# A new written-out order of steps and other filler products, in a kernel of banded attention and a Mish layer

## The chip, the cores and the metric

The kernel runs on one core of a Trainium2 chip. The metric is the time of one execution on the device in microseconds (us). TensorE multiplies matrices, VectorE (DVE), ScalarE (ACT) and GpSimd (POOL) work on elements, and SyncE (SP) issues the loads and stores to the DMA engines. Each engine works through its own list of instructions in order, and waits in that list for what it needs from others.

## The reference

```python
B, H, S, D = 8, 8, 576, 64                       # q, k, v
scores = q @ k^T / sqrt(D)                       # heads 0-3: the last 32 keys
scores = where(mask, scores, -1e9)               # heads 4-7: every 4th of the last 128 keys
attn = softmax(scores) ; attn_out = attn @ v
x = attn_out as [B*S = 4608, H*D = 512]
h = x @ w_in                                     # 512 x 2048
g = h * tanh(log1p(exp(min(h, 20))))             # or h*tanh(h) above 20
out = g @ w_out                                  # 2048 x 512
```

The weights are 64-bit numbers: each of the two is 8 MB in HBM, and is loaded as integers and turned into a pair of f16 numbers (a high and a low half) on the chip.

## The kernel before

The work is cut into 16 units (u = 0 to 15), half a sequence of 288 rows each. The attention of a unit is small: scores of two kinds (0 plain band, 1 dilated), 72 and 96 f32 products of 64 by 32 by 64; exponentials; transposes; values in three parts; division; transposes of x. Units 0 to 2 ("direct") take their values as f32 and transpose on TensorE, later ones work with pairs of f16 and transpose by DMA. The hidden layer of a unit is eight steps of 24 products (128 x 128 by 288), each in two halves of 12. The output layer of units 0 to 2 is 16 steps of 12 products; for later units it is replaced by seven products of sums of quarters, on sums of w_out that VectorE makes once (su, gq, ga, fq).

The weights come in half groups of 1024 KB: w_in's group g as wl0.g.0 and wl0.g.1, w_out's as wl1.g.0 and wl1.g.1. Each half group goes through a maximum (wm on ACT or POOL, ws on TensorE and VectorE), through its words (ww: POOL, then VectorE twice) and through the split (wp: ACT, then VectorE). Four buffers hold loaded halves; w_in's group 1 goes straight into the room of w2.

Every step is a generator function that issues a piece of work, yields, and goes on when its name comes again. The order of all instructions is a list written out by hand of some 2120 names, ORDER (L41 to L175), which the loop at L1012 follows; a planner outside of the kernel has searched it. Each engine's list of instructions is what this loop issues to it, in that order. "=2" behind a name tells which of the buffers in turn is taken. The names, with the function and its lines: ld loads q, then k, then two halves of the dilated keys (loads, L455); lv loads values, plain and dilated in turn, first a memset for direct units (loads_v, L484); qp copies q (L481); sp, sc, ex, tp, va, tx are scores, maximum, exponential, transpose, values, transpose of x (L551, L580, L611, L637, L668, L717); pr finds the scale of v (L510); wl, wm, ws, ww, wp are the weights (L340 to L424); ff is a step of the hidden layer (L781); fo one of the output layer (L964); kw and kh multiply fillers.

In sc the units 0 and 1 subtract the maximum by a product on TensorE (L604). In lv the dilated values go by one DMA per window s into interleaved places of one tile (L503 to L506):

```python
for s in range(ns):
    row = vd[b, 0, half * (RB - K0) + s * step, 2 * a * D:2 * (a + 1) * D]
    nc.sync.dma_start(o[:, n0:].rearrange("k (r s) n -> k r s n", s=ns)[:, :, s],
                      bass.AP(row.tensor, row.offset, [[w, WK], [2 * RB * w, NR], [1, 2 * D]]))
```

The fillers multiply ones into a spare corner of PSUM that nobody reads, "kw" n times in f32 (two products each), "kh" n times in bf16 (one each):

```python
def keep_warm(n, one=ones):
    for _ in range(n):
        nc.tensor.matmul(spare, one.broadcast_to([P, P]), one.broadcast_to([P, WIDE_MAX]), start=not spared, stop=True, skip_group_check=True)
```

## Time and profile before

| what | before |
|---|---|
| median of 3 runs | 860.55 us (857.65 to 860.93) |
| the profiled execution | 862.81 us, span 860.9 us |
| TensorE busy | 842.1 us, 98% of the span |
| VectorE, ScalarE, GpSimd busy | 636.1, 477.8, 96.0 us |
| mean granted clock of TensorE | 0.992 |
| DMA, mean over the span | 100 GB/s |

The span runs from the first to the last instruction of the profile. "PE" is TensorE's products, "PEld" its weight loads, "SPq" the load queue of SyncE. A granted clock of 1.00 is 2.4 GHz, 0.50 is 1.2 GHz. A record in an engine's timeline may hold many instructions of one line; in brackets stands the idle time ahead of it and what ended it, and "issue" means that the engine waited for nothing that the profile shows. A few records of products are missing.

### The profile page before, as it was taken

Reading aid. Unit: us, or ns where it says so; the run is one execution under the profiler, and the core shown is the slowest. Engines: PE = TensorE matmul, PEld = TensorE weight load, DVE = VectorE, ACT = ScalarE, POOL = GpSimd, SP = SyncE. Lnnn points to the kernel's source line nnn. Section 1 sums busy time; section 2 is a strip of 40 time slices with the busy share of each in tenths; the row PEclk is TensorE's granted clock in tenths of the full one; section 3 lists DMA queues with packets and bytes.
Section 4 is the critical chain, followed back from the end, with each engine's and each line's share of the span. In section 5 each row is a group of like instructions: output and inputs, shape, how many; then the busy total and the mean of one; then the engine's idle time right before and its main releaser. Section 6 shows DMA issues by size and latency. Waiting matters only on the chain.

```text
span 860.9 us, 32197 instructions
## 1 busy us (share of the span) xinstructions
PE 842.1 (98%) x14818; PEld 727.3 (84%) x14821; DVE 636.1 (74%) x818; ACT 477.8 (55%) x615; POOL 96.0 (11%) x99
## 2 busy tenths in 40 slices
...
GB/s 270 213 151 266 154 146 87 73 144 130 70 57 13 126 80 178 57 144 96 126 67 102 69 150 76 131 72 102 94 73 109 43 127 18 57 40 34 1 22 37
DMA packets 154887, 86.29 MB, mean 100 GB/s; under 512 B 92288, under 2 KB 150656, under 8 KB 154752
## 3 DMA queue, kind: packets, MB, share of 16 engines
...
q8 instruction: 116, 1.90, 1.0%
...
## 4 chain that ended last, share of the span: by engine, by line
PE 86%; DMA 7%; DVE 3%; SPq 2%; ACT 1%; issue 1%; POOL 0%; DVEq 0%; POOLq 0%; ACTq 0%
PE b L790 40%; PE b L933 31%; PE b L972 8%; DMA vf<-in_vd 4%; PE b L689 4%; PE b L577 3%; DMA raw<-in_w_in 2%; DMA knd<-in_kdT 1%; DVE g L903 1%; SPq L348 1%; DVE hm L909 0%; DVE w L424 0%; SPq L501 0%; PE b L385 0%; ACT g L901 0%
## 5 line engine op out<-in xcount | busy, mean ns | idle before, releaser
L790 PE MATMUL b<-x,w 128*128 128x288 f16 x3072 | 393.4, 286 | 0.2 <-ACT hm L796 0.2
L790 PEld LDWEIGHTS <-w 128*128 128x128 f16 x3072 | 295.4, 98 | 75.5 <-issue 0.6
L903 DVE SCALAR_TENSOR_TENSOR g<-hm,sg,g 128x1152 f16<-128x1152 f32 (+1 forms) x104 | 131.3, 1272 | 53.7 <-ACT g L901 52.9
L933 PE MATMUL b<-g,w 128*128 128x144 f16 x2496 | 164.9, 226 | 0.8 <-issue 0.7
L933 PEld LDWEIGHTS <-w 128*128 128x128 f16 x2496 | 158.4, 98 | 3.2 <-issue 1.1
L796 ACT ACTIVATE hm<-b,fs 128x576 f32<-128x576 f32 x128 | 92.8, 738 | 113.5 <-PE b L790 99.2
L901 ACT ACTIVATE g<-hm,sg 128x1152 f16<-128x1152 f32 (+1 forms) x104 | 116.0, 1127 | 40.1 <-PE b L933 26.4
L481 POOL COPY qp<-qn 128x576 f32<-128x576 f32 x15 | 34.9, 2326 | 433.6 <-DMA qn<-in_qT 317.9
L909 DVE TENSOR_TENSOR hm<-hm 128x576 f32<-128x576 f32 x104 | 79.0, 763 | 1.9 <-ACT hm L796 0.4
L972 PE MATMUL b<-g,w 128*128 128x288 f16 x576 | 73.3, 286 | 0.1
L947 ACT ACTIVATE y<-b,fo 128x288 f32<-128x288 f32 x52 | 40.6, 786 | 58.9 <-PE b L933 57.6
L972 PEld LDWEIGHTS <-w 128*128 128x128 f16 x576 | 55.6, 98 | 14.4 <-DVE w L424 0.3
L952 DVE SCALAR_TENSOR_TENSOR y<-b,fo,y 128x144 f32<-128x144 f32 x78 | 33.6, 478 | 45.8 <-PE b L933 22.7
L933 PE MATMUL b<-g,g 128*128 128x144 f16 x936 | 66.6, 226 | 0.3 <-DVE y L952 0.2
L933 PE MATMUL b<-g,late_sums 128*128 128x144 f16 x936 | 65.9, 226 | 0.0
L933 PEld LDWEIGHTS <-g 128*128 128x128 f16 x936 | 60.6, 98 | 2.2 <-issue 0.6
L933 PEld LDWEIGHTS <-late_sums 128*128 128x128 f16 x936 | 60.0, 98 | 0.5
L727 ACT CAST x<-xs 96x512 f16<-96x512 f32 (+1 forms) x39 | 26.7, 686 | 30.9 <-DMA x<-x 17.1
L729 DVE TENSOR_TENSOR x<-xs,x 96x512 f16<-96x512 f32 (+1 forms) x39 | 30.1, 772 | 16.6 <-ACT x L727 16.4
L545 DVE SCALAR_TENSOR_TENSOR vh<-vn,s,vh 128x2688 f16<-128x2688 f32 (+1 forms) x13 | 35.2, 2705 | 8.6 <-ACT vh L543 8.6
L705 DVE TENSOR_TENSOR xs<-b,rec 96x512 f32<-96x512 f32 (+1 forms) x48 | 37.2, 776 | 4.4 <-DVE rec L703 0.5
L689 PEld LDWEIGHTS <-pT 64*32 64x32 f16 (+1 forms) x3276 | 30.2, 90 | 5.3 <-issue 3.6
(127 smaller groups left out, 821.1 us busy)
## 6 DMA issues: line engine op xcount, KB each, us to landing
...
```

The source lines that it names most:

```text
L481: nc.gpsimd.tensor_copy(qp.rearrange("p (b r i) -> p b r i", r=NR, i=SQ // NR), d["q"][:, :2 * HT].rearrange("p (b i r) -> p b r i", r=NR, ...
L545: nc.vector.scalar_tensor_tensor(lo, src, s, hi, ALU.mult, ALU.subtract)
L689: nc.tensor.matmul(avv[s * SQ:(s + 1) * SQ, a, t - t0, h * (D + 1):(h + 1) * (D + 1)], p, vv[vi][ks, v0:v0 + D + 1], start=(i == 0), stop= ...
L705: nc.vector.tensor_tensor(xs.rearrange("p (a t h e) -> p a t h e", a=2, h=2, e=D), avv[:, :, :, 1:AW - 1].rearrange("p a t (h e) -> p a t ...
L790: nc.tensor.matmul(ph[:, h, :HT], w1[j][:, c, wi, k * P:(k + 1) * P], x_of(d, xi, c), start=(n == 0), stop=(n == len(seq) - 1))
L796: nc.scalar.activation(d["m"][p][:, half, k0:k0 + 2], ph[:, :, :HT], AF.Mish, scale=d["fs"][:, j:j + 1])
L901: nc.scalar.activation(hi, src, AF.Identity, scale=sg)
L903: nc.vector.scalar_tensor_tensor(lo, src, sg, hi, ALU.mult, ALU.subtract)
L909: nc.vector.tensor_tensor(a, a, b, op=op)
L933: nc.tensor.matmul(acc[e], left(l, e, p, wi)[:, k * P:(k + 1) * P], right(gi, k), start=(n in opens and p == 0 and q == 0), stop=(last and ...
L947: nc.scalar.activation(into(half, t), by(acc), AF.Identity, scale=fo)
L972: nc.tensor.matmul(po[:, :HT], w2[:, e, j, wi, k * P:(k + 1) * P], d["g"][j][:, gi, k, :], start=(j == 0 and n == 0), stop=(j == NCH - 1 a ...
```

## The change

Only the text of ORDER is changed: 2122 names instead of 2123. All steps other than the fillers occur as often as before; they are listed in another order, with other buffers in turn. The fillers before are kw18, kh32, kw17, kw8, kw1, kw3 and kw1; after, they are kw6, kh102, kw1, kw2, kw2 and kw2. The front of both lists and their last lines:

```diff
@@ -39,139 +39,138 @@
 EPS = 1.0e-9
 
 ORDER = """
-ld0 ld0 wl0.3.0 lv0 mf cs0 qp0 ww0.3.0 xa0 cs1 wl0.3.1 xa1 kw18 kh32 sp0.0=0 wm0.3.0 ld0 mf lv0 ww0.3.0 ld0 wm0.3.0
-wl0.0.0 wm0.3.1 lv1 ww0.3.0 sp0.0 wl0.0.1 ww0.3.0 ww0.3.1 kw17 sp0.1=1 sc0.0 ww0.0.0 sp0.1 ww0.3.0 ww0.3.1 lv0
-ww0.3.1 ws0.3=2 sc0.1 wm0.0.0 ws0.3 lv0 ww0.0.0 ww0.3.0 ld1 ww0.0.1 ww0.0.0 sc0.0 sc0.1 wm0.0.1 ex0.0 ld1 wp0.3.1
-kw8 tp0.0=3 ww0.0.1 wp0.3.1 kw1 ws0.0=2 ex0.1 ld1 ws0.0 ww0.0.1 qp1 wp0.0.0 tp0.1=0 kw3 sp1.0=1 tp0.1 sp1.0 ld1 lv0
-sp1.1=2 sp1.1 lv1 wp0.0.1 wl0.1.0 tp0.0 wp0.0.0 sc1.0 sc1.0 sc1.1 pr0 sc1.1 pr0 va0.0=0 wl0.1.1 wp0.3.0 pr0=3 pr0
-ex1.1 va0.0 va0.1=3 ww0.1.0 va0.0 wp0.3.0 va0.1 ex1.0 va0.2=2 lv1 va0.2 lv1 va0.0 va0.1 tp1.1=1 va0.1 wl0.2.1
-wm0.1.0 va0.2 fs0.0 tx0.1=3 va0.0 va0.2 wm0.1.1 tp1.1 kw1 tx0.0=0 ww0.1.0 tx0.1 ww0.1.1 lv1 tx0.0 tp1.0=2 ww0.1.1
-tp1.0 tx0.2=1 tx0.1 wl0.2.0 ws0.1=2 tx0.2 tx0.0 ld2 tx0.2 ww0.2.1 ff0.6=3 ff0.6 wp0.0.1 ws0.1 wm0.2.1 ww0.1.1
-ff0.7=0 wp0.1.1 ff0.0=1 ww0.2.0 ff0.0 fs0.3 ww0.1.0 ff0.1=2 lv2 ff0.7 ww0.2.1 wp0.1.1 wp0.1.0 ww0.2.1 wl1.1.0 fs0.1
-wp0.1.0 ff0.0 pr1 ff0.1 lv2 ff0.7 ff0.6 ff0.1 va1.2=1 wm0.2.0 pr1 va1.2 va1.0=0 va1.0 ld2 va1.0 pr1=3 ld2 ff0.2=2
-ww1.1.0 pr1 va1.2 ff0.2 ww0.2.0 va1.2 va1.0 ws0.2=3 ww0.2.0 ff0.2 ff0.3=1 ws0.2 tx1.2=2 ld2 tx1.2 ff0.3 wp0.2.0
-va1.0 wp0.2.1 tx1.0=3 tx1.2 wp0.2.0 wp0.2.1 sp2.1=0 wm1.1.0 va1.1=2 sp2.1 ff0.3 wl1.1.1 va1.1 tx1.0 tx1.0 ff0.5=1
-ww1.1.1 va1.1 sc2.1 ff0.4=3 wm1.1.1 qp2 ft wl1.0.0 wl1.0.1 fs0.4 fs0.2 va1.1 ww1.1.0 wm1.0.0 ff0.5 ff0.4 tx1.1=0 fs1
-sp2.0=2 ff0.5 ww1.1.1 tx1.1 tx1.1 ff0.4 sp2.0 gt0.0=0 ff1.0=1 gt0.1=1 lv2 sc2.0 ws1.1=0 ww1.1.1 ww1.0.0 ff1.6=3
-ws1.1 lv2 ff1.7=2 ex2.0 ff1.7 wp1.1.1 wp1.1.1 gt0.2=2 gt0.0 ff1.0 ff1.2=0 gt0.3=3 gt0.3 ld3 ex2.1 ff1.6 wm1.0.1 lv2
-ld3 wl1.2.0 ww1.0.1 ff1.2 ff1.0 ww1.2.0 ff1.6 ff1.7 ww1.0.0 ff1.1=1 ww1.1.0 gt0.1 wp1.1.0 ld3 ff1.5=3 xa2 ff1.1
-ff1.1 ww1.0.0 ww1.0.1 tp2.0=2 wp1.1.0 wl1.2.1 tp2.0 ws1.0=1 gt0.2 ws1.0 ff1.5 wp1.0.0 tp2.1=2 ww1.0.1 ff1.2 wp1.0.0
-ff1.4=1 wm1.2.0 wp1.0.1 tp2.1 ff1.5 ff1.4 pr2 ff1.3=0 pr2 ww1.2.0 ff1.4 ff1.3 wm1.2.1 ww1.2.1 fo0.0.0=2 wp1.0.1
-wl1.3.0 ff1.3 ww1.2.1 wl1.3.1 ww1.3.0 pr2=3 wm1.3.0 fo0.0.1 ws1.2=1 va2.2=0 pr2 va2.1=3 fo0.0.2 ws1.2 fo0.0.3
-fo0.0.3 ww1.2.0 va2.2 va2.0=1 va2.0 va2.2 va2.0 va2.1 xa3 fo0.1.0 wm1.3.1 fo0.1.1 ww1.2.1 va2.1 fo0.1.2 wp1.2.0
-va2.0 fo0.1.3 wp1.2.1 gt1.0=4 va2.1 va2.0 fs2 gt1.3=5 fo0.0.3 ww1.3.1 gt1.1=6 wp1.2.0 fo0.2.0=3 ld3 fo0.1.3 tx2.1=1
-fo0.2.1 ww1.3.1 ww1.3.0 ws1.3=2 wp1.2.1 va2.2 tx2.0=0 ww1.3.0 ws1.3 tx2.0 fo0.2.2 qp3 tx2.2=2 ww1.3.1 tx2.0 fo0.2.3
-fo0.1.3 sp3.1=0 sp3.1 tx2.1 wp1.3.0 fo0.2.3 wp1.3.0 tx2.1 fo0.3.0 fo0.3.1 tx2.2 wp1.3.1 wp1.3.1 fo0.3.2 ol fo0.3.3
...
-fq14.6.1 ga15.0 gq15.0.3 fq15.1.0=0 fq14.6.1 ga15.1 ga15.0 gq15.1.0 fq15.0.1 fq14.4.1 ga15.1 gq15.0.2=0 fq15.1.1
-gq15.1.3=1 gq15.1.3 fq15.0.1 fq15.2.0 fq14.4.1 ga15.1 gq15.0.2 fq15.2.1 fq15.1.1 gq15.1.2=4 gq15.1.2 fq15.2.1
-fq15.3.0 fq15.3.1 fq15.3.1 fq15.4.0 fq15.5.0 fq15.5.1 fq15.4.1 fq15.5.1 fq15.4.1 fq15.6.0 fq15.4.1 fq15.6.1 fq15.6.1
-fq15.6.1
+wl0.0.1 mf wl0.0.0 ww0.0.1 ww0.0.0 cs1 ld0 ld0 lv0 wm0.0.1 wm0.0.0 ww0.0.1 qp0 wl0.3.0 kw6 kh102 sp0.0=0 cs0 mf ld0
+sp0.0 lv0 ww0.0.0 ws0.0=1 ww0.0.1 xa0 ld0 xa1 sc0.0 sc0.0 wm0.3.0 ww0.0.0 ex0.0 wl0.3.1 lv0 sp0.1=2 ws0.0 wm0.3.1
+wm0.3.0 ww0.3.0 sp0.1 ww0.3.0 wp0.0.1 ww0.3.0 lv0 tp0.0=3 sc0.1 tp0.0 wp0.0.0 ww0.3.0 ld1 ww0.3.1 ld1 sc0.1 ww0.3.1
+ex0.1 ld1 ww0.3.0 lv1 kw1 ws0.3=1 wp0.0.1 kw2 tp0.1=0 ld1 wp0.0.0 ws0.3 kw2 sp1.1=2 ww0.3.1 tp0.1 wp0.3.1 sp1.1
+ww0.3.0 sc1.1 qp1 lv0 sp1.0=3 wl0.1.0 kw2 sc1.1 wp0.3.1 sp1.0 va0.1=1 ex1.1 wm0.1.0 pr0 lv1 pr0 ww0.1.0 sc1.0 pr0=0
+wp0.3.0 pr0 va0.1 va0.1 va0.0=2 wl0.1.1 sc1.0 va0.0 ex1.0 va0.0 va0.0 va0.2=0 ww0.1.0 va0.2 va0.2 ww0.1.1 va0.1
+wm0.1.1 tp1.1=3 va0.0 tx0.1=1 wp0.3.0 tp1.0=2 tp1.1 tx0.0=3 va0.2 tx0.1 fs0.0 wl0.2.1 wm0.2.1 ww0.1.1 tx0.2=0 tx0.1
+lv1 lv1 tp1.0 tx0.0 tx0.0 ww0.2.1 ws0.1=2 tx0.2 tx0.2 ff0.0=1 ww0.2.1 ws0.1 ww0.1.0 ff0.7=3 ff0.1=0 wp0.1.0 wl0.2.0
+ww0.1.1 wm0.2.0 ff0.6=2 ff0.0 ff0.6 ww0.2.0 wp0.1.0 ww0.2.1 wp0.1.1 ff0.0 fs0.1 ww0.2.0 wp0.1.1 lv1 ld2 ff0.7 ff0.1
+ws0.2=1 ww0.2.0 fs0.3 ws0.2 lv2 ff0.7 ff0.2=3 ff0.2 va1.0=1 ft ff0.6 va1.0 va1.0 wp0.2.1 pr1 ff0.1 va1.2=2 pr1 ld2
+va1.2 ff0.2 pr1=0 ff0.3=3 pr1 va1.0 ff0.3 va1.2 va1.0 wl1.1.0 qp2 va1.2 wp0.2.0 ld2 tx1.0=0 wp0.2.1 ld2 tx1.0
+tx1.2=1 sp2.1=2 wm1.1.0 ff0.3 wl1.1.1 sp2.1 lv2 va1.1=3 tx1.2 wp0.2.0 va1.1 tx1.2 ff0.5=1 fs0.4 va1.1 fs0.2 ww1.1.0
+gt0.0=0 va1.1 gt0.1=1 tx1.0 ff0.5 wm1.1.1 wl1.0.0 ff0.4=3 ff0.4 gt0.3=2 sc2.1 tx1.1=0 ww1.1.1 ff0.4 sp2.0=2 gt0.3
+tx1.1 fs1 ff0.5 gt0.2=3 tx1.1 sp2.0 ff1.5=3 ww1.1.0 ld3 ff1.5 lv2 ww1.1.1 ff1.2=0 sc2.0 ex2.1 ws1.1=1 ff1.2 gt0.0
+ws1.1 wl1.0.1 tp2.1=2 lv2 ff1.2 ff1.3=1 ww1.1.1 ww1.1.0 gt0.2 ff1.3 wp1.1.0 wm1.0.0 ld3 lv2 wp1.1.0 ff1.0=0 xa2
+ww1.0.0 ww1.0.1 ff1.5 ex2.0 tp2.1 ff1.0 ww1.0.0 ff1.3 pr2 wm1.0.1 ww1.0.1 ff1.4=3 ff1.4 wl1.3.1 gt0.1 wp1.1.1
+ww1.0.0 ff1.0 ld3 ws1.0=2 ff1.1=1 ff1.7=0 ff1.4 wp1.1.1 ff1.7 ws1.0 gt1.2=4 ff1.6=3 ff1.6 tp2.0=2 ww1.3.1 pr2
+wp1.0.0 ff1.7 ff1.6 wp1.0.0 fo0.0.0=0 ww1.0.1 ff1.1 wl1.2.1 tp2.0 pr2=3 wp1.0.1 ff1.1 fo0.0.1 va2.0=2 gt1.2 va2.0
+va2.0 va2.2=1 ld3 wp1.0.1 gt1.1=5 pr2 va2.1=3 va2.2 va2.1 va2.0 wm1.3.1 gt1.0=6 qp3 va2.0 wl1.2.0 va2.1 fo0.0.2
+fo0.0.3 va2.2 tx2.0=2 fo0.0.3 ww1.3.1 va2.1 tx2.0 gt1.0 tx2.1=3 wl1.3.0 va2.2 gt1.3=7 tx2.0 fo0.1.0 tx2.2=1 tx2.2
+ww1.2.1 ww1.2.0 fo0.1.1 wm1.2.1 wm1.2.0 tx2.2 sp3.1=2 ww1.3.0 fo0.0.3 tx2.1 sp3.1 tx2.1 ff2.2=1 sc3.1 gt1.1 ff2.0=3
+fo0.1.2 ww1.2.1 ff2.2 ww1.3.1 fs2 ff2.0 gt1.3 wm1.3.0 ld4 ww1.2.0 fo0.1.3 ff2.2 ex3.1 fo1.0.0=2 ww1.2.1 ff2.0
+fo1.0.1 fo0.1.3 ws1.2=1 ww1.3.0 ww1.3.0 ws1.2 fo1.0.2 ww1.2.0 fo1.0.3 wp1.2.0 fo1.0.3 ff2.3=3 ws1.3=0 ff2.1=1 ws1.3
+wp1.3.0 ff2.1 ff2.6=0 ff2.1 ff2.3 ff2.7=1 wp1.2.0 fo1.0.3 ff2.6 wp1.3.0 ff2.7 wp1.2.1 wp1.3.1 wp1.3.1 ff2.3 mr=3
...
+gq15.1.1 ff15.3 gq15.0.0 ga15.0 ff15.3 fq15.0.0=2 fq15.1.0=0 gq15.1.1 ga15.0 ga15.1 fq14.6.0 fq14.6.1 gq15.1.0=1
+gq15.0.3=4 gq15.1.0 ga15.1 gq15.1.3=2 ga15.0 ga15.1 gq15.1.3 gq15.0.2=3 gq15.0.3 fq15.0.1 ga15.1 fq15.1.1 gq15.0.2
+fq14.6.1 fq15.0.1 fq15.2.0 fq15.2.1 fq15.1.1 gq15.1.2=1 fq15.3.0 gq15.1.2 fq14.6.1 fq15.2.1 fq15.3.1 fq15.3.1
+fq15.4.0 fq15.5.0 fq15.5.1 fq15.4.1 fq15.5.1 fq15.6.0 fq15.4.1 fq15.6.1 fq15.4.1 fq15.6.1 fq15.6.1
 """.split()
```

## Rows read from the trace of the kernel before

**Rows 1.** The page, part 1: busy time, share and instructions of each engine.

```profile
PE 842.1 (98%) x14818; PEld 727.3 (84%) x14821; DVE 636.1 (74%) x818; ACT 477.8 (55%) x615; POOL 96.0 (11%) x99
```

**Rows 2.** Busy time by stretch: length, PE, PEld, DVE, ACT, POOL, clock, DMA share, GB/s.

```profile
100.00:140.00 40.00, 38.06 (x580) 31.02 (x578) 38.15 (x55) 20.48 (x29) 29.09 (x13) 1.00 0.32 98
140.00:840.00 700.00, 698.91 (x12597) 610.63 (x12595) 519.08 (x653) 402.13 (x514) 28.66 (x36) 1.00 0.39 85
```

**Rows 3.** Groups of fillers by form, windows 0 to 9.7 and 9.7 to 50 us.

```profile
L999 PE MATMUL b<-ones 128*128 128x96 f32 x36 | 7.6, 408 | 0.9 <-DVE ln_p L991 0.9
...
L999 PE MATMUL b<-ones 128*128 128x96 f32 x60 | 7.8, 281 | 0.0
```

**Rows 4.** TensorE in order of time, 0 to 60 us: start, length, instruction.

```profile
0.92 9.02 PE L999 MATMUL b<-ones 128*128 128x96 f32 x68 [0.92 <-DVE ln_p L991]
9.78 0.49 PE L565 MATMUL b<-m_b,ident_p 96*96 96x384 bf16 x2
...
15.49 0.86 PE L577 MATMUL b<-knd,qn 64*32 64x64 f32 x44
18.30 1.28 PE L577 MATMUL b<-knd,qn 64*32 64x64 f32 x52 [1.95 <-issue]
...
28.00 0.82 PE L659 MATMUL b<-ident,sb 96*128 96x96 f32 x8
...
30.41 0.97 PE L577 MATMUL b<-knp,qp 64*32 64x64 f32 x72 [0.60 <-POOL qp L481]
...
31.88 1.20 PE L577 MATMUL b<-qk 64*32 64x64 f32 x73
34.38 0.44 PE L577 MATMUL b<-qk 64*32 64x64 f32 x23 [1.30 <-issue]
...
38.54 1.11 PE L689 MATMUL b<-vf,pp 64*32 64x65 f32 x71
42.98 1.57 PE L689 MATMUL b<-vf,pp 64*32 64x65 f32 x73 [3.33 <-issue]
44.48 1.54 PE L659 MATMUL b<-ident,sb 96*128 96x96 f32 x8
...
50.66 9.59 PE L790 MATMUL b<-x,w 128*128 128x288 f16 x77
```

**Rows 5.** TensorE in order of time, 60 to 150 us, four of its waits.

```profile
67.97 1.06 PE L382 MATMUL b<-w,ones 128*128 128x512 bf16 x3 [0.88 <-DVE w L413]
...
73.74 0.33 PE L577 MATMUL b<-knd,qn 64*32 64x64 f32 x12 [0.38 <-DMA knd<-in_kdT]
75.51 0.57 PE L577 MATMUL b<-knd,qn 64*32 64x64 f32 x35 [1.43 <-DMA knd<-in_kdT]
...
117.97 0.61 PE L385 MATMUL b<-w,ones 128*128 128x128 bf16 x8 [0.69 <-DVE w L413]
```

**Rows 6.** Busy time by stretch, two short stretches behind waits (columns as in rows 2).

```profile
42.00:50.00 8.00, 6.58 (x104) 6.12 (x105) 5.39 (x9) 5.85 (x11) 1.13 (x1) 0.57 0.19 55
76.00:80.00 4.00, 4.00 (x116) 3.04 (x105) 2.99 (x5) 0.35 (x1) 1.72 (x2) 0.57 0.99 326
```

**Rows 7.** The load queue in order of time: issues of dilated values.

```profile
12.50 0.60 SPq L505 DMA_DIRECT2D vf<-in_vd  x1
...
22.71 0.60 SPq L505 DMA_DIRECT2D vf<-in_vd  x1
...
26.54 0.61 SPq L505 DMA_DIRECT2D vf<-in_vd  x1
...
32.53 0.60 SPq L505 DMA_DIRECT2D vf<-in_vd  x1
```

**Rows 8.** ScalarE's, then the weight loads' order of time: first work on landed loads.

```profile
12.57 1.12 ACT L370 ACTIVATE w<-raw 128x1024 f32<-128x1024 f32 x1 [2.27 <-DMA raw<-in_w_in]
...
32.23 0.70 PEld L577 LDWEIGHTS b<-qk 64*32 64x32 f32 x62 [0.18 <-DMA qk<-in_kdT]
```

**Rows 9.** Instruction transfers: whole run, then 15.4-15.8 and 39.9-40.3 us.

```profile
q8 instruction: 116, 1.90, 1.0%
...
q8 instruction: 1, 0.02, 17.3%
...
q8 instruction: 1, 0.02, 16.2%
```

210 lines of the change are left out of this document (104 added, 106 removed).

## The prediction

> **What bounds the kernel now.** The first view is the busy times: TensorE works in 98% of the span [rows 1]. The second is the busy time by stretch: from 140 to 840 us TensorE is idle for 1.1 us of 700 [rows 2]. There the end is set by the sum of the products, which the change leaves as they are; another order can lose there, hardly win. What a new order can win lies ahead of 140 us, and the third view, TensorE in order of time, tells where. Three kinds of loss stand there. (a) TensorE does nothing of use until 9.78 us, when the first loads are in; until then it multiplies fillers [rows 4]. (b) Between 9.78 and 50.66 us, where the first product of the hidden layer starts, much of the time is waiting or filler: 60 f32 fillers take 7.8 us [rows 3], and the waits put down to "issue" ahead of 18.30, 34.38 and 42.98 us are 1.95, 1.30 and 3.33 us [rows 4]. (c) Behind 50.66 us it waits 0.88 us for words of weights, 0.38 and 1.43 us for keys of unit 2, and 0.69 us for VectorE [rows 5].
>
> Behind such waits the clock falls to the lower of its two levels, 1.2 of 2.4 GHz: the mean granted is 0.57 from 42 to 50 us and 0.57 from 76 to 80 us [rows 6]. Eight transposes of scores take 0.82 us at 28.00 and 1.54 us at 44.48 [rows 4].
>
> Two more views say why. In the issues of the load queue each second load of dilated values (in_vd) is issued only when the one before it has landed, and that one lies behind all that was queued earlier: 12.50 to 22.71 us, and 26.54 (behind the loads of unit 1) to 32.53 us [rows 7]. So the values of unit 0 are whole at about 36 us, and nothing of the hidden layer can start much earlier than the work behind them. Then the instruction transfers: the counts of the first 6, 19 and 24 rows of TensorE's timeline (the last of each stand in [rows 4]) add up to 222, 476 and 603 products, so the three "issue" waits stand on multiples of 127 products from 95. 116 transfers of 1.90 MB in all carry the 14818 products and 14821 weight loads, so 256 instructions or some 127 products each [rows 1, 9]. The transfer that ends the wait at 18.30 leaves at 15.4, that of 42.98 at 39.9 [rows 9], so it is in some 3.0 us after leaving. By its place it is asked for when TensorE passes the boundary before: 95 products were passed at about 10.4 us, 476 at 34.38, which makes 5.0 and 5.5 us of queueing, each time behind loads just issued; where little was queued (349 passed at about 30.7, resumed at 34.38) the whole took 3.7 us. The Trainium skill, Runtime: NRT & Kernel Launch, section Instruction fetch mechanics, has the same blocks of 256 instructions, but calls the cost of crossing one "mostly hidden"; the trace has 6.6 us in three places, and by that rule the change would have none of it to win or to lose.
>
> **The change, part by part.** (1) Fillers. f32 ones fall from 48 calls (96 products) to 13 (26), short ones rise from 32 to 102. In front stand 12 f32 products instead of 36. These 36 took 7.6 us [rows 3], the 32 short ones the rest to 9.78 us, under 0.05 each. So the new front lasts 2.5 us plus 102 times 0.05 (clock up) to 0.1 us (clock down): it ends between 8.5 and 13.6 us. A filler costs nothing where TensorE would have waited; what it guards is the clock, and behind the front the new order keeps 14 of 60 f32 products.
>
> (2) Front of the load queue. The weights of group 0 (2048 KB) now stand ahead of the queries and keys of unit 0. Down to those keys 2.84 MB are queued; before, the first 2.84 MB ended with a half of group 3's weights, and these were in at 12.57 us [rows 8]. So the first scores start at 12.5 to 13 us, not 9.78. The end does not feel it: ahead of the first load of dilated values both orders queue the same 5.4 MB, and from there to the second such load (26.54) the same loads. Keys of unit 1 land at 32.2 us in either [rows 8]. The small steps of unit 0 in between took 19 us before, 10 without fillers and waits, and have 13 to 32 us. Where that cover is gone (all of them at half clock) they end at 33, 1 us late.
>
> (3) From 32.2 us to the first hidden product. In the new order 326 products are done when unit 1's dilated scores (98) start, so boundary 349 is passed at about 32.4 us with little queued; the next block is in 3.5 to 3.7 us later, at 35.9 us, and TensorE, at 476 since about 34.3, waits some 1.6 us. The next 127 products are of the kinds of before (eight maximum products, rests of scores, four pieces of values), which took 34.38 to 39.65 us, 5.3 us, so 603 is reached at 41.2 us. The block asked for at 35.9 us queues behind weights and values issued from 33.2 on (1024, 288 and up to 1024 KB, with 1024 KB more behind). I take 5.2 us, between the two seen, and 3.0 behind it: 44.1 us. What is left to the first hidden product is the list of before, 42.98 to 50.66, 7.7 us at the lower clock, less two filler products (0.5 us): 51.3 us against 50.66. So +0.6 us. Bounds: with nothing queued no wait, and 2.7 us less for the clock, 45.7 us; with 7 us of queueing 53.
>
> (4) Behind it. The second half of group 2's weights is queued ahead of, no longer behind, the last dilated values of unit 1, and unit 2's keys no longer behind unit 2's first values. By the sizes these keys are in at about 68 us; TensorE comes to them some 21 us behind the first hidden product (12 half-steps of the hidden layer at 1.5 us, as 77 products take 9.59, five pieces of values at 0.37, as 71 take 1.11 [rows 4], and transposes), at 72. So the 0.88, 0.38 and 1.43 us go, and with them the low clock from 76 to 80 us, which at 0.57 granted costs 1.7 us: -4.4 us. The maxima of w_out's group 3 stand some 12 us of products later than before, so the 0.69 us goes too: -0.7 us.
> What comes in: between boundaries 857 and 984 the new order has four pieces of values and two half-steps, 5 us of work, where before had four half-steps, 8 us; behind 984 both have 2.3 us up to 1111. A block needs 3.7 to 8.5 us. Bounds of the two waits together: 0, and 6.6 us, the sum of the three seen. I take two of the smallest seen, 2.6 us, since the load queue is often short behind dilated values.
>
> (5) The steady part is reordered all through. Its products are the same and it was idle for 1.1 us: 0, with bounds -1 and +4 (its idle time five times over). The last products and stores stand as before.
>
> Sum: 0.6 - 4.4 - 0.7 + 2.6 + 0 = -1.9 us on a span of 860.9. The profiled execution took 862.81 us, 2.3 over the median of 860.55; taken from the median that gives 858.6 us.
>
> **The rivals.** A, the transfers come in time: the block for 603 finds a short queue, the clock stays up, and the first hidden product starts at 45.7 us, 5.6 earlier than forecast: 853.0 us. With only the two later waits gone: 856.0. For it: the queue alone decides, and 1024 KB less in it is worth 3 us. Against it: from 33.2 us on more is issued without a stop than before. The skill's "mostly hidden" would be this case; three rows speak against it.
> B, the late transfers move to the scores of unit 2, and the kernel gets slower: if over 1 MB is queued when 857 products are passed (about 66 us, behind three loads of weights), TensorE waits 2.6 us at 984 and 4.0 us at 1111, and the clock falls behind them, 1.5 us more: 8.1 instead of 2.6 us, 864.1 us, 3.6 over before; with the clock low from 13 us on, for want of fillers, 1 to 3 us on top, up to 867. For it: 35 filler calls fewer and a denser run of small products. Against it: before, TensorE waited there for keys, not for instructions.
> C, the change does not do what it says: the waits at 476 and 603 stay, as I hold too, and what is won behind 50 us VectorE takes back, which is busy for 38.15 of 40 us from 100 to 140 [rows 2]: no difference, 860 to 861.
>
> **How the numbers follow.** Forecast and C together 0.46, A in full or in part 0.35, B 0.19. Predicted: 858.6 us. The range reaches from A's full case to B without the low clock in front: 852.5 to 864.8. 0.5% is 4.3 us, about what a measurement of this kernel can tell from no change. Below 856.25 lies A, with a little of the forecast's own spread; above 864.85 the upper part of B and of the steady part's bound. Faster 0.36, same 0.46, slower 0.18.
>
> **What would show it.** In the changed kernel's trace: first scores at 12.5 to 13 us and unit 1's keys at 32; "issue" waits at 476 and 603 products that end near 35.9 and 44.1; the first hidden product at 51.3; no wait for unit 2's keys and none for words of weights near 63 us; TensorE idle under 2 us from 140 to 840. The prediction is wrong if the first hidden product comes before 48 or after 53 us, or if the steady part is idle for more than 4 us.

## The result, and the profile after

The changed kernel takes 866.01 us (median of 13 runs, 862.72 to 870.43), the kernel before 860.5 beside it (857.65 to 863.82): ratio 1.0077, interval 1.0056 to 1.0099 (from all runs of both; the two medians alone are 5.5 us, or 0.64%, apart). It is slower by 0.8%, above the forecast of 858.6 and above its range. The profiled execution took 870.11 us (span 868.3), so it lies at the upper end of its runs, as the one of before (862.81) does; sizes below are those of these executions, and where a size differs from run to run this is said. Line numbers are one lower than before's; the later kernels have theirs three or four lower still.

Busy time of TensorE, from the page of after (before: [rows 1]):

```profile
PE 837.1 (96%) x14821; PEld 721.6 (83%) x14821; DVE 628.7 (72%) x818; ACT 480.2 (55%) x615; POOL 90.8 (10%) x99
```

Busy time by stretch of after, columns as in [rows 2] and [rows 6]; the last line is the end of the kernel:

```profile
42.00:50.00 8.00, 5.04 (x102) 4.71 (x103) 5.49 (x8) 5.15 (x10) 4.37 (x2) 0.79 0.42 147
...
80.00:86.00 6.00, 5.10 (x48) 3.43 (x48) 4.05 (x6) 3.98 (x5) 4.58 (x3) 0.72 0.49 167
...
100.00:140.00 40.00, 39.94 (x579) 32.25 (x578) 36.73 (x45) 25.45 (x33) 20.27 (x9) 1.00 0.42 136
140.00:840.00 700.00, 692.98 (x12514) 605.59 (x12513) 510.87 (x658) 396.04 (x507) 24.93 (x40) 1.00 0.39 84
840.00:869.00 29.00, 24.02 (x385) 23.83 (x382) 14.04 (x18) 10.62 (x12) 0.00 (x0) 0.96 0.09 33
```

The same end in the trace of before:

```profile
840.00:861.00 21.00, 17.01 (x273) 16.82 (x270) 7.22 (x10) 4.68 (x6) 0.00 (x0) 1.00 0.09 31
```

From 100 to 140 us TensorE lost 1.94 us before [rows 2] and loses 0.06 now. From 140 to 840 it was idle for 1.09 us [rows 2] and now is for 7.02. That is 5.9 of the 7.4 us between the two spans. Of the rest 0.4 us are waits behind 840 us (span less 840 us less TensorE's busy time there: 3.9 us before, 4.3 now), and 1.1 us stand ahead of 140 us: there TensorE has 717.0 us of work left (692.98 and 24.02), before 715.9 (698.91 and 17.01). TensorE of after in order of time, the lines that answer to [rows 4, 5]:

```profile
12.28 0.97 PE L576 MATMUL b<-knp,qp 64*32 64x64 f32 x72 [2.28 <-POOL qp L480]
...
30.50 1.08 PE L576 MATMUL b<-qk 64*32 64x64 f32 x84 [0.38 <-DMA qk<-in_kdT]
...
34.43 0.24 PE L998 MATMUL b<-ones 128*128 128x96 f32 x1 [1.22 <-issue]
...
43.74 1.46 PE L688 MATMUL b<-vf,pp 64*32 64x65 f32 x74 [3.96 <-issue]
...
50.94 9.23 PE L789 MATMUL b<-x,w 128*128 128x288 f16 x74
...
64.52 1.06 PE L381 MATMUL b<-w,ones 128*128 128x512 bf16 x4 [1.66 <-ACT hm L795]
...
74.33 0.55 PE L737 MATMUL b<-ident,xs 96*128 96x96 f32 x4 [0.36 <-issue]
...
80.90 0.45 PE L688 MATMUL b<-vf,pp 64*32 64x65 f32 x23 [4.23 <-issue]
```

The waits put down to "issue" stand behind 477, 605, 986 and 1113 products, within two of the block boundaries that the forecast worked with (476, 603, 984 and 1111; a few records are missing). The first hidden product comes at 50.94 us (50.66 before). The keys of unit 2 are waited for no more; in place of that stands the wait of 4.23 us, and the clock behind it is 0.72 from 80 to 86 us, 1.7 us lost. So ahead of 140 us gains and losses nearly balance, at 1.1 us of loss. Behind it three waits of some size are new, in TensorE's order of time:

```profile
195.73 0.18 PE L329 MATMUL b<-m,ones 128*128 128x2 bf16 x1 [0.90 <-DVE m L322]
...
349.62 1.64 PE L789 MATMUL b<-x,w 128*128 128x288 f16 x12 [2.78 <-DVE xs L704]
...
454.52 1.75 PE L789 MATMUL b<-x,w 128*128 128x288 f16 x13 [2.38 <-issue]
```

The second stands behind 5536 products. Its releaser is VectorE, and VectorE in order of time tells what held it:

```profile
343.64 0.82 DVE L322 TENSOR_REDUCE m<-vn 128x1 bf16<-128x640 f32 x1 [3.13 <-DMA vn<-in_v]
345.45 1.22 DVE L521 TENSOR_REDUCE m<-vn 128x1 bf16<-128x1024 f32 x1 [0.98 <-DMA vn<-in_vd]
...
348.88 0.69 DVE L704 TENSOR_TENSOR xs<-b,rec 96x512 f32<-96x512 f32 x1
```

It sat 4.1 us in front of values of unit 7 that had not landed, and the division that frees TensorE's bank stood behind that in its list. The load queue of after has those loads behind a transposing transfer and a load of keys:

```profile
335.73 1.65 SPq L651 DMA_TRANSPOSE pT<-p  x1
337.42 1.48 SPq L474 DMA_DIRECT2D knd<-in_kdT  x1
338.95 0.63 SPq L500 DMA_DIRECT2D vn<-in_v  x1
339.63 1.96 SPq L504 DMA_DIRECT2D vn<-in_vd  x3
```

The third stands behind 7627 products, on a block boundary. Ahead of it the scores of unit 10 of both kinds run together, TensorE in order of time:

```profile
446.84 0.45 PE L688 MATMUL b<-vh,pT 56*32 56x65 f16 x36
447.18 0.71 PE L576 MATMUL b<-knp,qp 64*32 64x64 f32 x48
447.69 1.11 PE L576 MATMUL b<-knd,qn 64*32 64x56 f32 x94
...
449.02 3.11 PE L789 MATMUL b<-x,w 128*128 128x288 f16 x24
```

Counted back 128 products from the wait, the block ahead of it begins in the third of these lines, near 447.8 us. Over 100 of its products are short ones, so with the 24 long ones at its end it lasts only some 4.3 us (to 452.13). The next block is there at 454.52, some 6.7 us after this one began, and loads of values and a transposing transfer are issued in between.

### The profile page after: what moved, and what is told of

Its sections match the earlier page's. It is cut to its first block, busy times and chain, and to the rows that moved or that the text cites. A ratio compares the mean times of both kernels' runs of the same rounds, so it can differ in the third digit from the quotient of the medians.

```text
span 868.3 us, 32213 instructions
## 1 busy us (share of the span) xinstructions
PE 837.1 (96%) x14821; PEld 721.6 (83%) x14821; DVE 628.7 (72%) x818; ACT 480.2 (55%) x615; POOL 90.8 (10%) x99
## 4 chain that ended last, share of the span: by engine, by line
PE 83%; DMA 7%; DVE 3%; SPq 3%; issue 2%; ACT 1%; POOL 0%; DVEq 0%; ACTq 0%; POOLq 0%
PE b L789 39%; PE b L932 29%; PE b L971 7%; PE b L688 3%; PE b L576 3%; DMA raw<-in_w_in 3%; DMA vf<-in_vd 2%; DMA vn<-in_vd 1%; SPq L504 1%; DMA out_T<-y 1%; DVE hm L908 1%; SPq L500 1%; SPq L474 1%; DMA x<-x 0%; SPq L347 0%
## 5 line engine op out<-in xcount | busy, mean ns | idle before, releaser
L480 POOL COPY qp<-qn 128x576 f32<-128x576 f32 x15 | 23.3, 1556 | 452.6 <-DMA qn<-in_qT 318.9
L971 PEld LDWEIGHTS <-w 128*128 128x128 f16 x576 | 55.6, 98 | 14.5 <-issue 0.2
L728 DVE TENSOR_TENSOR x<-xs,x 96x512 f16<-96x512 f32 (+1 forms) x39 | 30.1, 771 | 24.1 <-ACT x L726 24.1
L542 ACT ACTIVATE vh<-vn,s 128x2688 f16<-128x2688 f32 (+1 forms) x13 | 29.7, 2281 | 11.5 <-DVE s L318 9.8
```

What stands on the lines that cost most here:

```text
L728: nc.vector.tensor_tensor(lo, xs, hi, op=ALU.subtract)
L971: nc.tensor.matmul(po[:, :HT], w2[:, e, j, wi, k * P:(k + 1) * P], d["g"][j][:, gi, k, :], start=(j == 0 and n == 0), stop=(j == NCH - 1 a ...
```

## The experiments

One table for all of them. "Idle" is 700 us less TensorE's busy time from 140 to 840 us in the profiled execution of each, the reading of [rows 2]. The kernel before was timed again beside each group of runs (medians 859.26 to 860.54 us); the ratios, and the last column, are against that.

| run | zeros, against before | median us | ratio to before, 95% interval | idle us | median over that of before, us |
|---|---|---|---|---|---|
| before | 128 | 860.5 | 1 | 1.09 | 0 |
| after | same | 866.01 | 1.0077, 1.0056 to 1.0099 | 7.02 | 5.5 |
| e1 after's front | same | 864.85 | 1.0055, 1.0032 to 1.0078 | 2.96 | 4.3 |
| e2 before's front | same | 862.86 | 1.0034, 1.0013 to 1.0055 | 3.04 | 2.3 |
| e3 after | +23 | 884.60 | 1.0278, 1.0247 to 1.0309 | 24.53 | 24.1 |
| e4 before | +24 | 872.53 | 1.0138, 1.0109 to 1.0167 | 11.25 | 12.0 |
| e5 before | +128 | 862.41 | 1.0022, 1.0007 to 1.0036 | 2.21 | 2.8 |
| e6 before | +24, +104 later | 862.65 | 1.0029, 1.0016 to 1.0042 | 1.33 | 3.0 |
| e7 after, 2 places | same | 864.40 | 1.0055, 1.0036 to 1.0075 | 4.99 | 4.8 |
| e8 e7 and loads | same | 866.46 | 1.0083, 1.0061 to 1.0106 | 3.94 | 6.8 |
| e9 before | -104 | 871.31 | 1.0130, 1.0105 to 1.0154 | 8.86 | 11.0 |
| e10 e7 | -105 | 874.77 | 1.0182, 1.0151 to 1.0213 | 12.18 | 14.5 |
| e11 after | +128 | 870.82 | 1.0108, 1.0073 to 1.0143 | 6.17 | 10.5 |
| e12 before, short zeros | same | 859.85 | 1.0003, 0.9988 to 1.0018 | 0.72 | -0.5 |
| e13 before, weights | same | 860.48 | 1.0018, 1.0003 to 1.0032 | 0.78 | 1.2 |
| e14 after, 4 places | same | 864.25 | 1.0060, 1.0045 to 1.0075 | 3.43 | 5.0 |
| e15 e13 and keys | same | 860.46 | 1.0012, 0.9998 to 1.0025 | 0.62 | 1.2 |
| e16 before, no zeros | -128 | 860.19 | 1.0017, 1.0001 to 1.0033 | 0.87 | 0.9 |

Where the loss is large (e3, e4, e9, e10, 11 to 24 us) 70 to 97% of it is idle time of the stretch that the forecast put at 0. In the other kernels up to 5.4 us (e11) are left over: the idle time is that of one execution, and it holds neither what a low clock costs nor what is lost ahead of 140 us.

**Which half of the order costs (e1, e2).** The two lists are cut near the first hidden product and joined crosswise.

```diff
-before: all of its list
+e1: after's list up to name 504, then what is left in before's order, 12 buffer numbers renamed
+e2: before's list up to name 508, then what is left in after's order, 2 buffer numbers renamed
```

> The changed order's first 504 names, which reach to about 170 us, and behind them the steps that are left in the order of the kernel before (12 buffers in turn taken otherwise). Theory 'two places': of the 5.5 us the front holds about 2 (a wait of 4.2 us ahead of product 1113 for instructions, against waits for keys before) and the steady part about 4, so this kernel takes 862 to 863 us and its steady part is idle for 1 to 2 us from 180 to 840. Rival 'all in front': the waits behind 170 us are late consequences of the front, so the time stays at 865 to 867 us and waits of 2 us and more stand behind 170 us.

> The front of the order before (508 names, to about 170 us), and behind it the steps that are left in the changed order. Theory 'two places': the steady part's waits at 340 to 360 and 440 to 460 us (2.8 and 2.4 us) stand here too, 864 to 865 us. Rival 'all in front': 860 to 861 us and no wait over 1 us behind 170 us.

Measured: e1 +4.3 us, e2 +2.3 us over before, both between the two theories. e2 has the wait behind 5536 products again (2.63 us), and none behind 7627. In e1 1.9 of the 4.3 us are idle time behind 140 us (the largest piece 1.30 us, the wait of after's 195.73). Both halves cost, after's front no less than its steady part, and neither theory's number held.

**Blocks against work: 24 products of zeros more or fewer (e3, e4).**

```diff
-kh102        (after)
+kh125        (e3)
-kh32         (before)
+kh56         (e4)
```

> The changed kernel with 125 instead of 102 short fillers in front, where TensorE waits from 9.5 to 12.3 us anyway. Theory 'blocks of instructions': the long waits stand at counts of products (477, 605, 1113), so they move 23 products forward in the steps; boundary 349 is then passed ahead of the wait for unit 1's keys, the wait at 477 goes, that at 605 shrinks under 1 us, one of 2 to 4 us may stand at about 731, the first hidden product comes at about 48 instead of 50.9 us, and the wait at 1113 falls to 1 to 3 us: 860 to 863 us. Rival 'places': the waits belong to the steps they stand at (the second piece of unit 0's values, the second of unit 1's), stay there with 4 us each, and the time stays at 866.

> The kernel before with 56 instead of 32 short fillers in front, nothing else. Theory 'blocks of instructions': the wait of 3.3 us ahead of product 603 goes from the values of unit 0; the block of boundary 349 is asked for at about 29 us, ahead of the wait for unit 1's queries; one wait is left near 730 counted products, ending at about 46 us, and the first hidden product comes at about 47 instead of 50.7 us: 856 to 858 us. Rival 'places': the waits stay at their steps, 860 to 861 us, or 1 us more for the longer front.

In the front the waits that the theory named went: neither kernel has one of over 0.1 us ahead of the first values' products, and the first hidden product comes at 48.13 us in e4 (50.66 before) and 48.85 in e3 (50.94 after). How much of that is the boundary's doing is not shown, since e12 comes to 48.37 us with the boundary and its wait in place. But e4 lost 12 us against before and e3 18.6 against after, which neither theory nor rival had, and the losses lie hundreds of microseconds from the edit. TensorE of e4 in order of time, six waits:

```profile
224.34 1.89 PE L785 MATMUL b<-x,w 128*128 128x288 f16 x14 [0.97 <-issue]
...
287.75 0.47 PE L928 MATMUL b<-g,late_sums 128*128 128x144 f16 x5 [1.36 <-issue]
...
340.38 1.88 PE L785 MATMUL b<-x,w 128*128 128x288 f16 x14 [1.19 <-issue]
...
410.90 2.31 PE L785 MATMUL b<-x,w 128*128 128x288 f16 x14 [3.27 <-issue]
...
474.53 0.86 PE L928 MATMUL b<-g,g 128*128 128x144 f16 x11 [1.69 <-issue]
...
488.30 0.61 PE L928 MATMUL b<-g,late_sums 128*128 128x144 f16 x7 [1.61 <-issue]
```

All are "issue" waits on block boundaries: the counts of products ahead of them differ by multiples of 127 to 128. The products of zeros shift every later boundary against the work, and at some of the new places the next block is late.

**A whole block more, or fewer (e5, e9, e16).** If it is the shift, then 128 products more or fewer, one block, must leave the steady part as it is.

```diff
-kw18 kh32 ... kw17 ... kw8 ... kw1 ... kw3 ... kw1    (before, 128 products)
+kw18 kh160 ... kw17 ... kw8 ... kw1 ... kw3 ... kw1   (e5, 256)
+kw8 ... kw1 ... kw3                                   (e9, 24)
+none                                                  (e16, 0)
```

> The kernel before with 160 short products of zeros in front in place of 32: 128 more, which is one instruction block of TensorE by the distance of the issue waits (127 to 128 products). Theory (what 24 more did to the steady part, 12 us, was the phase of the blocks against the work): the steady part from 140 us on is as before, with 1 to 2 us of idle time and not 11; first scores at about 15.9 us and not 9.78; first hidden product within 1 us of 50.7, since loads set the pace until 32 us; 860 to 863 us in all. Rival (a longer stretch of zeros in front costs by itself, whatever its count): worse than the 872.5 us that 24 more gave, 872 to 880 us, with the steady part idle for over 8 us.

> The kernel before with 24 products of zeros in all in place of 128: those ahead of the first scores and between them are gone (kw18, kh32, kw17 and one kw1), and kw8, kw1 and kw3 behind the scores stay. 104 fewer is 24 more by the phase of blocks of 128, so theory: the front goes as with 24 more (no issue wait of 3.3 us ahead of the first values' products, first hidden product near 48.1 us), the steady part idles for 1 to 2 us as before, and no fillers are paid: 857 to 859.5 us. What the lower clock costs the first scores hides behind the loads until 30 us. Rival (the zeros in front hold the clock that the front needs): clock at half speed in the stretch from 30 to 50 us, first hidden product at 50.5 us or later, 860.5 to 864 us.

> The kernel before without any product of zeros: 128 fewer than it has, a whole block by the phase, where the run with 24 of them had 104 fewer. Theory (phase decides, the zeros themselves hardly matter): from 140 us on it idles for 0.5 to 2.5 us as before, and not for 8.9 as with 24 left; the first scores run at the low clock, behind loads; the issue wait ahead of the first values' products is there as before (at 475 to 477 products now); 859.5 to 862.5 us. Rival (fewer zeros are what cost 11 us in the run with 24): 870 us or more, steady part idle for over 8 us.

e5 came out close to its theory (862.4 us, idle 2.2 for 1 to 2, first hidden product at 52.22, half a microsecond later than allowed), though it has five times the added zeros of e4. The expectation of e9 contradicts itself: 104 fewer is 24 more by the block, so its steady part had to be that of e4, not that of before. And so it came. TensorE of e9 in order of time, three of its six waits:

```profile
222.54 1.65 PE L785 MATMUL b<-x,w 128*128 128x288 f16 x12 [0.93 <-issue]
...
406.80 2.37 PE L785 MATMUL b<-x,w 128*128 128x288 f16 x18 [1.28 <-issue]
...
482.65 0.61 PE L928 MATMUL b<-g,late_sums 128*128 128x144 f16 x7 [1.87 <-issue]
```

These are e4's waits, at the same lines and 131 products earlier in the count (3281 for 3412, 6730 for 6861, 8137 for 8268; the lists differ by 128, and the trace of e9 lacks a few records). With e9 alone the loss could still be put down to missing zeros. e16 settles that: none at all, and the steady part is that of before, by stretch:

```profile
140.00:840.00 700.00, 699.13 (x12618) 611.21 (x12616) 520.27 (x654) 402.62 (x515) 27.41 (x36) 1.00 0.39 85
```

So leaving out all 128 products of zeros costs 1.5 us by the ratio (0.1 to 2.8 by the interval), and leaving out 104 of them costs 11 us: the boundaries decide, not the zeros.

**Keeping the front's gain (e6, e10).**

```diff
-kh32 ... ws0.2 ... sp2.0 ... ws1.2                       (before)
+kh56 ... kh46 ws0.2 ... kh26 sp2.0 ... kh32 ws1.2        (e6)
-kw6 kh102                                                (after)
+kh9                                                      (e10, with the two places of e7)
```

> The kernel before with 56 short products in front in place of 32, and 104 more behind the first hidden product: 46 ahead of the weight scale ws0.2, 26 ahead of the scores sp2.0, 32 ahead of the scale ws1.2, each where TensorE waited. So 128 more in all, and the blocks of the steady part stand as before. Phase theory: the front's gain stays (first hidden product near 48.1 us and not 50.7), the fillers cost 0 to 3 us where TensorE waits in part, the steady part from 140 us on idles for 1 to 2 us: 858 to 862 us. Rival (phase is not what the steady part hangs on): it idles for 8 us or more as with 56 alone, 868 to 875 us.

> The kernel after with both places of the steady part changed as in the run a_steady, and with 23 products of zeros in all in place of 128 (nine short ones ahead of the first scores, the kw1 and three kw2 behind them): 105 fewer is 23 more by the phase. Theory: from 140 us on the kernel idles for what the steady changes alone left if the blocks are 128 products apart, 3 to 5 us, the front loses its issue waits ahead of the first values' products, and the time is 861 to 863.5 us. Rival (phase does not carry the front's gain, or the clock falls): 864.5 us or more. As many products as this part of the order was searched with are not there, so a miss of one product at a boundary may show as a wait of up to 2 us.

e6: first hidden product at 48.41 us, steady idle 1.33: the phase (where the boundaries fall in the work) did what the theory said, but the total is 1.0029 of before. The 104 products are 5 us of work at 0.05 us each, which may have taken back the 2.3 us; that was not tried apart. e10 makes the mistake of e9: 105 fewer is 23 more, so its steady part is of e3's kind (12.2 us idle).

**After's steady waits: do they belong to the order (e11)?**

```diff
-kh102        (after)
+kh230        (e11)
```

> The kernel after with 230 short products of zeros in front in place of 102, 128 more. Theory (the waits of its steady part belong to the order and the phase of blocks): the waits ahead of products 5536 and 7627 stand 128 products further on, at 5664 and 7755, the first of 1 to 3 us and the second of 2 to 2.5 us, and the steady part idles for 4 to 7 us; first hidden product within 1.5 us of 50.9, 866 to 869 us. Rival (they came of the one profiled run): neither is there, or under 0.5 us, and the steady part idles for under 2 us.

They are there, 128 products further on but for missing records (behind 5660 and 7751), TensorE of e11 in order of time:

```profile
348.94 1.38 PE L785 MATMUL b<-x,w 128*128 128x288 f16 x5 [3.70 <-DVE xs L700]
...
454.63 1.63 PE L785 MATMUL b<-x,w 128*128 128x288 f16 x12 [0.64 <-issue]
```

The place stays, the size does not: 2.78 and 3.70, 2.38 and 0.64. The steady part idles for 6.2 us, as the theory said, while the median of 870.8 us is above its 869. The longer one costs more than its length. Busy time by stretch of e11, TensorE alone (length, busy, clock, DMA share, GB/s):

```profile
349.00:351.00 2.00, 2.00 (x9) 0.50 0.14 32
351.00:353.00 2.00, 2.00 (x16) 0.50 0.00 0
353.00:355.00 2.00, 2.00 (x22) 0.73 0.46 107
```

The clock is at its lower level behind it, 2.5 us lost; behind the 2.78 us of after it stayed up. The length of the wait does not tell which: behind the shorter one of e2, at the same place, the clock fell too. TensorE of e2, the wait, then the stretch behind it:

```profile
343.60 1.96 PE L786 MATMUL b<-x,w 128*128 128x288 f16 x12 [2.63 <-DVE xs L701]
...
345.00:347.00 2.00, 2.00 (x17) 0.50 0.00 0
```

With 5.1 us more idle time than before and these 2.5 us, some 3 of the 10.5 us by which e11 is slower are not explained.

**Mending the places (e7, e14).**

```diff
@@ unit 7's values (e7, e14)
-tp6.1 ld8 ... lv7 lv7 ...
+lv7 tp6.1 lv7 ld8 ...
@@ scores of unit 10 (e7, e14)
-sp10.0 fq6.6.1 tx8.2 ff7.7 gq7.0.3 ff7.6 ff7.6 ff7.7
+fq6.6.1 tx8.2 ff7.7 gq7.0.3 ff7.6 ff7.6 ff7.7 sp10.0
@@ e14 alone
-pr7 pr7 ... va6.2 gq5.0.3
+pr7 ... va6.2 pr7 gq5.0.3
-va13.2 gq11.0.2 ... va13.2 fq11.2.0 fq11.2.1 fq11.1.1
+fq11.2.0 fq11.2.1 fq11.1.1 va13.2 gq11.0.2 ... va13.2
-pr4 gt2.2 tp4.0 fo1.2.3
+gt2.2 tp4.0 fo1.2.3 pr4
```

> The kernel after with two places of its order changed behind 300 us. Place one: the loads of unit 7's second values are put ahead of the transposing transfer tp6.1 and of the load ld8, as in the order before. Place two: the last 24 products of the scores sp10.0 are put behind four feed-forward pieces, so that the block of instructions that holds them lasts some 2.7 us longer ahead of its boundary at product 7627. Theory: the waits of 2.8 us ahead of product 5536 and of 2.4 us ahead of 7627 go, the steady part idles for 2 us and not 7, and the time is 860 to 862.5 us. Rival (the waits only move, since what is behind them is as late): under 1.5 us gained, 864.5 to 866.5 us, with a new wait of 2 us or more near either place.

> The kernel after with four places of its steady part changed: the two of the run a_steady, and two more that it left. The maximum of unit 7's values over the second part is taken behind the release of the bank that TensorE waits for at product 5532; three pieces of the quadratic form are run ahead of the last value products of unit 13, so that the block ahead of product 11714 lasts longer; the product of unit 4's maximum runs one feed-forward piece later (product 2769). Theory (the extra time of after is idle time of its steady part, place by place): from 140 us on it idles for 1 to 2 us and not 5 (7.0 in after), and the time is 860.5 to 863 us. Rival (the front is what costs, or a mended wait comes back elsewhere): 864 us or more, with the steady part under 2 us in the first case and still over 3 us in the second.

e7 took the wait behind 7627 products away and cut the other, and a third place came up, from TensorE's order of time:

```profile
344.13 1.64 PE L785 MATMUL b<-x,w 128*128 128x288 f16 x12 [0.95 <-DVE xs L700]
...
657.62 1.22 PE L928 MATMUL b<-g,w 128*128 128x144 f16 x17 [1.65 <-issue]
```

e14 mended that one as well, and a wait for ScalarE took its place some 50 products on:

```profile
658.76 1.66 PE L928 MATMUL b<-g,late_sums 128*128 128x144 f16 x24 [1.48 <-ACT den L694]
```

Idle time fell from 7.0 to 5.0 and 3.4 us, the ratio from 1.0077 to 1.0055 and 1.0060, with intervals that overlap: no gain in time is shown. The rivals' numbers (about 864.5 us) came true, in part through their second reason, waits that come back elsewhere. That the wait for unit 7's values belongs to its place in the order holds: it is 2.63 to 3.70 us in three traces without the edit (e2, after, e11) and at most 1.79 in e7, e8 and e14, with it. For the wait behind 7627 products that is not shown: it is gone with its edit in all three, but e2 has none and e11 0.64 us without it. That the steady part is all that makes after slow does not hold: e14 idles there for 2.3 us more than before and is 5.0 us slower, and of e7's 4.8 us 3.9 are idle time.

**Loads in front of instruction transfers (e8, e13, e15).**

```diff
@@ e8: after with e7's places
-ff0.3 wl1.1.1 sp2.1 ... wm1.1.1 wl1.0.0 ... ww1.1.1 ... ld3
+ff0.3 sp2.1 ... ld3 wl1.1.1 wl1.0.0 wm1.1.1 ww1.1.1
@@ e13, e15: before
-ld1 lv0 sp1.1 sp1.1 lv1 wp0.0.1 wl0.1.0
+ld1 wl0.1.0 lv0 sp1.1 sp1.1 lv1 wp0.0.1
@@ e15 alone
-lv2 ff0.7 ... ld2 ... ld2 ... ld2
+ld2 ld2 ld2 lv2 ff0.7 ...
```

> As the run before it, and the loads of weights wl1.1.1 and wl1.0.0 are put behind the load of unit 3's queries, with the words made of wl1.1.1 behind them: when TensorE passes 984 products (74.3 us) 1 MB less is queued ahead of the block that begins at 1113. Theory (that block came late because its transfer stood behind those loads): the wait of 4.2 us ahead of product 1113 falls to 0 to 1.5 us, and the low clock behind it, some 1.7 us, goes or shrinks: 856 to 859.5 us. Rival (the transfer is late for another reason, or the later words of wl1.1.1 make a wait of their own): within 1.5 us of the run before it.

> The kernel before with one thing moved: the load of weights wl0.1.0 (1 MB) stands ahead of the last step of unit 0's values, lv0, and not two steps behind it, so that it is issued near 26.5 us, when the load queue is about to run empty, and not at 33.9 us, just ahead of the request for the block that begins at product 603. Theory (that block was late because its transfer stood behind the loads issued from 33.2 to 36.0 us): its packet leaves at 35 to 37 us and not at 40.2, the issue wait of 3.33 us ahead of product 603 falls to under 1 us, the half clock from 42 to 49 us goes, the first hidden product comes at 47.5 to 48.5 us and not 50.66, and, no count being changed, the steady part idles for 1 us as before: 856.5 to 858.5 us. Rival (unit 0's values, 2.7 us later now, hold the first values' products instead, or the block is late for another reason): first hidden product at 50 us or later, 860 to 863 us.

> As the kernel before with the load of weights wl0.1.0 moved, and the keys of unit 2 loaded ahead of its values: the three steps of ld2 stand ahead of the values' load lv2, so that they are issued about 5 us earlier than at 67.5 to 69.4 us. Theory: beside what the moved weights give, the waits of 0.38 and 1.43 us for unit 2's keys go, which the kernel after shows too; 855 to 857.5 us, and 1 to 2 us below the run with the weights alone. Rival (TensorE then comes to the block boundary at 1111 products as much earlier, and waits for the transfer as the kernel after does): no gain over the run with the weights alone, an issue wait of 1 us or more at 984 or 1111 products.

e8, TensorE in order of time at the boundaries that follow 982 and 1109 products there:

```profile
74.06 0.55 PE L733 MATMUL b<-ident,xs 96*128 96x96 f32 x4 [1.01 <-issue]
...
77.88 0.45 PE L684 MATMUL b<-vf,pp 64*32 64x65 f32 x23 [1.48 <-issue]
```

The wait is 1.48 us and not 4.23, as the theory said. But e1, e7 and e14, with the loads where after has them, show 1.75, 1.75 and 2.03 there. From one boundary to the next TensorE has 2.3 us of work, and the next block took 3.82 us in e8 (74.06 to 77.88), while 0.16 MB were moved. In e1 and e7 it took 4.10 us each (73.88 to 77.98, 72.94 to 77.04), while about 1 MB was moved. So those loads are worth some 0.3 us to the block. In e11 it took 5.47 us, with 1.5 MB moved meanwhile, and in after 6.57, with 1.9; a longer time lets more through in any case, so what made it long in these executions is not shown. Nothing was gained: e8's median is 2.1 us above e7's, with intervals that overlap.

e13, then e15, TensorE in order of time at 476 and 603 products (1.30 and 3.33 us before [rows 4]):

```profile
36.00 0.44 PE L572 MATMUL b<-qk 64*32 64x64 f32 x23 [1.62 <-issue]
...
44.61 0.99 PE L684 MATMUL b<-vf,pp 64*32 64x65 f32 x73 [1.76 <-issue]
```

```profile
34.70 0.67 PE L572 MATMUL b<-qk 64*32 64x64 f32 x23 [3.70 <-issue]
...
43.24 0.99 PE L684 MATMUL b<-vf,pp 64*32 64x65 f32 x73 [0.33 <-issue]
```

e13's first hidden product comes at 51.34 us, 0.7 later than before: TensorE goes on at 476 products 1.6 us later than before, and the block behind 603 is asked for that much later. In e15, with the same loads ahead of 476, it waits there for 3.70 us. That would fit the moved load standing ahead of the transfer for the block behind 476; but these waits differ between executions by as much (none of over 0.6 us in e12 and e2, 1.30 before), so it is not shown. In both runs what one boundary gains the other gives back. The keys' waits went in e15 as its theory said, and a wait of 1.82 us behind 1110 products came, as its rival said: no gain over e13, and no difference from before.

**Short zeros for long ones (e12).**

```diff
-kw18 kh32        (before)
+kh68             (e12)
```

> The kernel before with 68 short products in front in place of 36 long and 32 short ones, the count kept: the part of the change that exchanges long zeros for short ones, alone. Theory: the first scores come at about 8 us (the long products take 0.21 us each at the low clock, the short ones less) or wait for their operands, the loads set the pace until 30 us, and every block boundary stays: 859.5 to 861.5 us. Rival (short zeros hold the clock less well): the clock at half speed in the first scores and later ones, first hidden product 1 us or more later, 861.5 to 864 us.

The scores start at 7.26 us and not 10.20, the first hidden product comes at 48.37, and the total is that of before. None of these kernels beats the kernel before by more than its interval.

## Why the prediction was wrong, step by step

(1) Fillers: right in that they cost the end next to nothing; e12 shows it of their kind (1.0003), e16 of their number (1.0017). What the step did not see is that each of them shifts every later block boundary. In the change itself this does no harm, since both lists have 128 in all.

(2) The front of the load queue: right in the main. First scores at 12.28 us (forecast 12.5 to 13; what came last was POOL's copy of the queries), hidden as said. The keys of unit 1 were there at 30.50 us, 1.7 earlier than forecast.

(3) The first hidden product: right for this execution, by luck in part. "Issue" waits behind 477 and 605 products, ending at 34.43 and 43.74 (forecast 35.9 and 44.1), first hidden product 50.94 (51.3). TensorE came to the second boundary at 39.78 us, 1.4 earlier than forecast, and the block took 9.3 us and not 8.2, so two errors cancel. And the price was taken for a constant, which it is not: the same front has 1.64, 1.49 and 0.39 us in place of 3.96 in e1, e7 and e14. The first hidden product, at 50.91, 49.70 and 48.42 there, does not follow this wait alone.

(4) Behind it: the second step that failed, a balance of the wrong size. The keys' waits (1.8 us) and the 0.69 us went. The 0.88 us for words of weights did not: 1.66 us stand there now, ended by a bank that ScalarE frees, since ScalarE waits in its order for weights of group 2. The two late transfers took 0.36 and 4.23 us, 4.6 and not 2.6, and the low clock came back behind them. So this was rival B's place, at 8.1 us by B, 6.3 by the trace (4.6 and 1.7 of clock). B's cause, more than 1 MB queued, is not shown: with those loads the block took 4.10 us in e1 and e7, without them 3.82 in e8. Steps 1 to 4 were to give -1.9 us; in the two traces after is 1.1 us behind at 140 us. Other executions vary there by more than that: the work left at 140 us is 712 to 716 us in e1, e7, e8 and e14, with after's front, and 713 to 716 in e12, e13, e15 and e16, with before's. A gain of 1.9 us does not show in them either.

(5) The steady part: the step that failed by most. "Its products are the same and it was idle for 1.1 us: 0, with bounds -1 and +4" was +5.9 us in the trace, past the 4 us of idle time that the prediction named as its sign of being wrong, and +5.1 us in the trace of e11. The argument counted work and took places for free. In their place the runs showed waits that belong to the order: for values loaded late (2.78 us, in e2 2.63, in e11 3.70) and, with a size that changes from one execution to the next, for a block of instructions behind short products (2.38 us, in e11 0.64, in e2 none). And they showed how much hangs on places: 23 or 24 products of zeros, which shift every boundary, cost either order 12 us or more. The trace of before could not show which place would miss; it did show 116 transfers, each with a boundary that any new order puts in front of other work, and the bound of +4 had no such row behind it. A tenth of a microsecond at each would have been 12 us.

The profiled span of 868.3 us is 9.3 over the forecast of 859.0 (860.9 less 1.9). 5.9 of that are step 5, 3.0 are steps 3 and 4 together, and 0.4 the waits behind 840 us.

What stays open: e1, after's front alone, came out 4.3 us over before, of which 1.9 are idle time behind 140 us. Where the other 2.4 are its trace does not show, nor why e14 keeps 5.0 us with 2.3 more of idle time. So whether the new front costs something, where the forecast had a gain, stays open. The halves cost 4.3 and 2.3, 6.6 together against 5.5 for the whole, which their intervals (2 us each way) allow. Why the same front's transfers take several microseconds more in some executions was not tried.

The Trainium skill, Runtime: NRT & Kernel Launch, section Instruction fetch mechanics, calls the cost of a block boundary "mostly hidden". That holds for most of the 116 boundaries here; the runs show single waits of 0.4 to 4.2 us at the others, and in the steady part of e3 18.0 of the 24.5 us of idle time are such waits, so here the measurement decides.
